# An attention, memory and expert kernel on one core: products of ones at the start, beta spread by TensorE, a shorter scaling, and tile changes counted in the plan

## The chip, the cores and the metric

The kernel runs on one core of a Trainium2 chip. The metric is the device time of one execution in microseconds, lower is better. The times of the kernel before are 636.03, 636.56 and 638.52 us; the median, 636.56 us, is the time that the change is measured against.

## The reference, cut to what matters

Four batches of eight heads, 576 positions of 64 values each, go through causal attention and, beside it, through a read of a memory matrix. A gate per head, the sigmoid of `beta`, mixes the two. The 2304 rows of 512 that come out pass through a gated expert of width 1536.

```python
a = softmax(causal(q @ k.T / 8));  local = a @ v            # 4 x 8 heads, 576 x 576, depth 64
mem_out = (phi(q) @ M_prev) / (phi(q) . z_prev + 1e-6)      # phi(x) = max(x, exp(min(x, 0)) - 1) + 1
g = 1 / (1 + exp(-beta))                                    # one number for each head
x = g * mem_out + (1 - g) * local                           # -> 2304 x 512
out = (sigmoid(x @ w_gate) * (x @ w_val)) @ w_out           # 512 -> 1536 -> 512
```

## The kernel before, in words

The 2304 rows are handled in six groups of 384 rows. Each group takes four pairs of heads, so that 24 pairs go through the attention. Group 0 and group 5 are "tail" groups: they hold the last 192 queries of two batches, with up to 576 keys; the four groups between hold the first 384 queries of one batch each.

A pair goes through these steps. `load_pair` (line 456) brings queries and keys, `load_values` (468) the values, `feature` (480) makes phi(q) on ScalarE and VectorE. `scores` (564) has TensorE multiply queries by keys: for the first nine pairs, and for one item of each pair of a tail group, through `heads` (555), which keeps 64-row tiles of the array busy side by side (fp32, line 560); for the others through split operands (line 315). VectorE adds the mask and finds the row extreme (line 597), ScalarE takes the exponential (606). `turn` (644) transposes the result, on TensorE for the first eight pairs (322), through a transposing DMA (617) between two VectorE copies (615, 619) for most of the others. `values` (666) multiplies by the values in products of 64 output rows (line 319, 66 columns), `memory` (508) does the memory read (319, 130 columns), and `scaled` (498) divides each result by its last column and multiplies it by the gate: four VectorE instructions, an addition of a small constant (501), a reciprocal (503), a product with the gate (504) and the large product (505); the helper line of the two last is 338. `across` (692) turns the mixed rows into the two halves `xh` and `xl` that the expert reads.

The expert, `moe` (818), runs over twelve slices of 128 columns of the width for each group; its matmuls are line 315. In the first group each slice's weights come from DRAM as 64-bit floats and are turned into two halves by `convert` (762) on ScalarE and VectorE (lines 769 to 780), through a ring of three landing buffers `wr`.

`gates` (376) makes the gates `gs` (the sigmoid of beta, for the memory) and `ga` (one less it, for the attention) from `bt`, a 128 x 8 tile into which one DMA (line 724) has copied the eight numbers of beta once for each partition: an exponential on ScalarE (377), an addition (378), a reciprocal (380) and a last pass (381) on VectorE.

No instruction is issued as the code is run through. Each is put in a list with its engine, a cost in microseconds and what it depends on (`Program.add`, line 80). `plan` (116) replays the list with these costs and gives every engine its order; `replay` (163) looks for time in which TensorE waits, and `issue` (198) makes 800 random trials that move late instructions forward, and keeps what is not worse. Each engine then runs its instructions strictly in the order found, SP's queue of DMAs too. In the costs, a TensorE instruction that starts before `COLD`, 8.0 us, costs half as much again, and a `heads` block carries 0.3 us on top of its columns.

```python
            if e == "pe":
                if at < COLD:
                    cost *= 1.5
```

Of the kernel before, what the change touches and what calls it, by code (L numbers as in the profile page):

```python
# [9 lines left out]
F32 = mybir.dt.float32  # L10
# [3 lines left out]
AF = mybir.ActivationFunctionType  # L14
ALU = mybir.AluOpType
# [14 lines left out]

WHEN = (20, 36)

COLD = 8.0

START = 0.7

# [15 lines left out]
class Program:  # L52
# [7 lines left out]
    def __init__(self):  # L60
        self.ops = []
        self.writer = {}
        self.readers = {}
        self.touched = {}
        self.before = {}
        self.closed = set()
        self.part = ""
        self.turn = None
        self.mates = []

    def renew(self, key):

# [43 lines left out]
    def plan(self, order):  # L116

        ops = self.ops
        left = [len(o[4]) for o in ops]
        ready_at = [0.0] * len(ops)  # L120
        engines = ["act", "dve", "pe", "pool", "sp"]
        free = dict.fromkeys(engines, START)
        link = 0.0
        coming = {e: [] for e in engines}
        ready = {e: [] for e in engines}
        for i, o in enumerate(ops):
            if not left[i]:
                heapq.heappush(coming[o[0]], (0.0, i))
        made = []
        for _ in ops:  # L130
            best = None
            for e in engines:
                if ready[e]:
                    at = free[e]
                elif coming[e]:
                    at = max(free[e], coming[e][0][0])
                else:
                    continue
                if best is None or at < best[0]:
                    best = (at, e)  # L140
            at, e = best
            while coming[e] and coming[e][0][0] <= at:
                k = heapq.heappop(coming[e])[1]
                heapq.heappush(ready[e], (order[k], k))
            i = heapq.heappop(ready[e])[1]
            _, cost, kb, _, _, _ = ops[i]
            if e == "pe":
                if at < COLD:
                    cost *= 1.5
            free[e] = at + cost  # L150
            done = free[e]
            if kb:
                link = max(link, done + WORLDS[0][1]) + kb / WORLDS[0][0]
                done = link
            made.append(i)
            for u in self.users[i]:
                ready_at[u] = max(ready_at[u], done + WAKE[e][ops[u][0]])
                left[u] -= 1
                if not left[u]:
                    heapq.heappush(coming[ops[u][0]], (ready_at[u], u))  # L160
        return made

    def replay(self, made, world):

        rate, lag, slips = world
        ops = self.ops
        ready_at = [0.0] * len(ops)
        start = [0.0] * len(ops)
        last = [-1] * len(ops)
        free = dict.fromkeys(WAKE, START)  # L170
        link = 0.0
        cold = COLD
        gaps = []
        for i in made:
            e, cost, kb, _, _, _ = ops[i]
            at = max(free[e], ready_at[i])
            if e == "pe":
                gap = at - free[e]
                if gap > 0.1:
                    gaps.append((gap, i))  # L180
                    if gap > 1.3:
                        cold = max(cold, at + 2.0)
                if at < cold:
                    cost *= 1.5
            elif e != "sp":
                cost *= slips[i]
            start[i] = at
            free[e] = done = at + cost
            if kb:
                link = max(link, done + lag) + kb / rate  # L190
                done = link
            for u in self.users[i]:
                t = done + WAKE[e][ops[u][0]]
                if t > ready_at[u]:
                    ready_at[u], last[u] = t, i
        return max(free.values()), gaps, start, ready_at, last
# [44 lines left out]
def tile_attention_memory_moe(  # L241
# [9 lines left out]
    nc = tc.nc  # L251
    B, HP, _, _ = qk.shape
# [54 lines left out]
        t, k = banks[ids[(turns[kind] - 1) % len(ids)]]  # L307
        return t, pg.renew(k)

    def pe(cost, emit, r, w):  # L310
        pg.add("pe", cost, emit, r, w)

    def matmul(out, lhsT, rhs, n, r, w, start, stop):
# [2 lines left out]

    def product(out, lhsT, rhs, n, r, w, start, stop):
        pe(0.068 if n <= 100 else 4 * n / 2385.0,
           lambda: nc.tensor.matmul(out=out, lhsT=lhsT, rhs=rhs, start=start, stop=stop), r, w)  # L319

    def transpose(out, in_, identity, r, w):
        pe(0.110, lambda: nc.tensor.transpose(out=out, in_=in_, identity=identity), r, w)  # L322
# [1 line left out]
    def act(n, emit, r, w):  # L324
        pg.add("act", 0.09 + n / 1200.0, emit, r, w)
# [4 lines left out]
    def dve(n, emit, r, w, fast=False):  # L330
        pg.add("dve", 0.065 + n / (1920.0 if fast else 960.0), emit, r, w)

    def pool(n, emit, r, w, fast=False):
        pg.add("pool", 0.2 + n / (950.0 if fast else 490.0), emit, r, w)
# [10 lines left out]
    def load(out, in_, kb, r, w):  # L345
        pg.add("sp", 0.5, lambda: nc.sync.dma_start(out=out, in_=in_), r, w, kb)
# [1 line left out]
    idn = sb.tile([128, 128], F32, name="idn")  # L348
    mask = sb.tile([128, 512], F32, name="mask")
    mask2 = sb.tile([128, 256], F32, name="mask2")  # L350
    bt = sb.tile([128, H], F32, name="bt")
    gs = sb.tile([128, H], F32, name="gs")
    ga = sb.tile([128, H], F32, name="ga")

# [19 lines left out]
            ), ["mask2"], ["mask2"])  # L374

    def gates():
        act(H, lambda: nc.scalar.activation(out=bt, in_=bt, func=AF.Exp, scale=-1.0), ["bt"], ["bt"])
        dve(H, lambda: nc.vector.tensor_scalar(
            out=gs, in0=bt, scalar1=1.0, scalar2=None, op0=ALU.add), ["bt"], ["gs"])
        dve(H * 8, lambda: nc.vector.reciprocal(out=gs, in_=gs), ["gs"], ["gs"])  # L380
        dve(H, lambda: nc.vector.tensor_scalar(
            out=ga, in0=gs, scalar1=-1.0, scalar2=1.0, op0=ALU.mult, op1=ALU.add), ["gs"], ["ga"])

    def half(t, k):
        r = slice(64, 128) if k[1] == 0 else slice(0, 64)
        pool(GT, lambda: nc.gpsimd.memset(t[r].bitcast(F32), 0.0), [], [k + ("z",)], fast=True)

    def pad(t, k):
        pool(64, lambda: nc.gpsimd.memset(t[:, S:], 0.0), [], [k + ("pad",)])
# [108 lines left out]
    def scaled(out, out_k, t, tk, ring, eps, gate, gate_k):  # L498

        r, rk = ring.take()  # L500
        dve(6, lambda: nc.vector.tensor_scalar(
            out=r, in0=t[:, :, :, D], scalar1=eps, scalar2=None, op0=ALU.add), [tk], [rk])
        dve(48, lambda: nc.vector.reciprocal(out=r, in_=r), [rk], [rk])
        tt(nc.vector, ALU.mult, r, r, gate.unsqueeze(1).to_broadcast([128, 3, 2]), 6, [rk, gate_k], [rk])
        tt(nc.vector, ALU.mult, out, t[:, :, :, :D], r.unsqueeze(3).to_broadcast([128, 3, 2, D]), GT,
           [tk, rk], out_k)

# [56 lines left out]
    def scores(n, c):  # L564
# [10 lines left out]
        def part(i, k0, k1):  # L575
            m = k1 - k0
            sp = [bank("att") for _ in js]
            if pair:
                es = [(0, 128, 0, 64), (1, 128, 64, 128)]
                mk, mk_k = (mask2[:, :m], "mask2") if i else (mask[:, :m], "mask")  # L580
            else:
                es = [(c if u.tail else 0, q0, 0, 128)]
                mk, mk_k = mask[:, 512 - W:], "mask"
            with pg.block():
                if n < SPLIT or pair:
                    pe(4 * m / 2385.0 + 0.3, lambda: heads(u, es, sp, js, k0, k1),
                       [u.kp[e][1] for e, *_ in es], [sp[j][1] for j in range(2)])
                for j in range(2) if n >= SPLIT and not pair else ():
                    for e, q, m1 in [(es[0][0], q0, 128)]:
                        kq, kk, ql, kx = u.kq[j][e]  # L590
                        keys = kq[:, u.ka + k0:u.ka + k1]
                        out, out_k = sp[j][0][:m1, :m], sp[j][1]
                        matmul(out, kq[:, u.qa + q:u.qa + q + m1], keys, m, kk, [out_k], True, False)
                        matmul(out, ql[:, q:q + m1], keys, m, kk + kx, [out_k], False, True)
            for j in range(2):
                (aj, ak), (sj, sk), (pj, pk) = a[j], st[j], sp[j]
                dve(m + 60, lambda aj=aj, sj=sj, pj=pj: nc.vector.tensor_tensor_reduce(  # L597
                    out=aj[:, k0:k1], in0=pj[:, :m], in1=mk, scale=-0.125,
                    scalar=3.0e38 if i == 0 else sj[:, i - 1:i],
                    op0=ALU.add, op1=ALU.min, accum_out=sj[:, i:i + 1],  # L600
                ), [pk, mk_k] + [sk] * (i > 0), [ak, sk])
# [115 lines left out]
    def attn():  # L717
# [3 lines left out]
        load_pair(1)  # L721
        feature(0)
        load_values(0)
        load(bt, beta.unsqueeze(0).to_broadcast([128, H]), 500, [], ["bt"])
        pg.part = "attention"
        load_values(1)
        late = []
# [167 lines left out]
    def step():  # L895
# [2 lines left out]
        pg.part = "expert"  # L898
        return y

    constants()
    a = attn()
    done = 0
# [81 lines left out]
```

## Time and profile before

| what | value |
|---|---|
| time, median of three executions | 636.56 us (636.03 to 638.52) |
| the profiled execution | 639.4 us |
| its span, first to last instruction | 637.6 us |
| TensorE matmuls busy | 620.8 us, 97% of the span |
| VectorE busy | 427.7 us, 67% |
| ScalarE busy | 301.9 us, 47% |

Busy time is the union of the recorded instructions of an engine. Matmuls overlap, so that a busy TensorE still holds short waits and slow starts. Times in the rows below count from the first instruction of the span. `PE` is TensorE's matmul, `PEld` its weight load, `DVE` VectorE, `ACT` ScalarE, `POOL` GpSimd, `SP` the engine that issues the DMAs. TensorE's two clock levels are 1.2 and 2.4 GHz; the column of the granted clock shows 1.00 for the higher one. That column is also 1.00 for a stretch ahead of the first record of the clock, so at the start the durations of matmuls of one size are the thing to read.

### The profile page before, as it was taken

The numbers are of one execution on the slowest core, as the hardware profiler recorded it, in microseconds if no ns is written. First come the engines' busy times: TensorE is split into PE (matmuls) and PEld (weight loads), VectorE is DVE, ScalarE is ACT, GpSimd is POOL, SyncE is SP. The second block draws the span as 40 slices with busy tenths as digits, with TensorE's granted clock in tenths as the row PEclk, the third lists the DMA queues.
The fourth block names the chain that finished last, engine by engine and source line by source line (L and its number), as shares of the span: only waits on it lengthen the run. The fifth ranks groups of instructions, "written<-read, shape, count | busy, mean of one in ns | idle before, by whom it ended". The sixth has DMA issues, their size and how long they took to land.

```text
span 637.6 us, 12197 instructions
## 1 busy us (share of the span) xinstructions
PE 620.8 (97%) x4740; PEld 547.2 (86%) x4740; DVE 427.7 (67%) x1164; ACT 301.9 (47%) x589; POOL 9.2 (1%) x51
## 2 busy tenths in 40 slices
PE   7989999999999989999999999999999999999997
PEld 3658888888999888899999999989898989999996
DVE  5799999999966767778767786779797422111211
ACT  5988677757743433534534643536353231221111
POOL 2000000000000000000000000000000000000000
PEclk9999999999999989999999999999999999999999
DMA  8567789895599988559867467779588433134442
GB/s 301 193 221 229 241 285 329 293 311 171 152 269 275 225 128 209 112 154 266 204 187 222 118 168 214 169 207 253 142 163 205 140 134 132 67 116 159 171 174 74
DMA packets 94362, 124.04 MB, mean 195 GB/s; under 512 B 70881, under 2 KB 72929, under 8 KB 87009
## 3 DMA queue, kind: packets, MB, share of 16 engines
q1 hardware_dynamic: 94160, 123.01, 67.8%
q8 instruction: 37, 0.61, 0.4%
q10 hardware_dynamic: 144, 0.26, 0.1%
q14 instruction: 21, 0.16, 0.1%
HBM read 89.43 MB, written 17.30 MB: 167 GB/s over the span
## 4 chain that ended last, share of the span: by engine, by line
PE 78%; DMA 10%; DVE 6%; ACT 4%; issue 1%; DVEq 0%; ACTq 0%; SPq 0%
PE bank L315 65%; PE bank L319 7%; DMA tl_wr<-pl_wr 5%; DMA wr<-in_w_dram 5%; PE bank L560 3%; PE bank L322 2%; ACT a L606 1%; ACT at L328 1%; ACT wt L769 1%; DVE wt L776 1%; DVE a L597 1%; DVE wt L773 1%; DVE pl_wr L615 1%; DVE at L619 1%; DMA kp<-in_qk_dram 0%
## 5 line engine op out<-in xcount | busy, mean ns | idle before, releaser
L315 PE MATMUL bank<-xh,wg 128*128 128x384 f32 x576 | 167.0, 343 | 0.1
L315 PE MATMUL bank<-xh,sv 128*128 128x384 f32 x576 | 163.8, 341 | 1.1 <-DVE th_a L861 1.1
L315 PE MATMUL bank<-sv,gh 128*128 128x512 f32 x432 | 138.3, 398 | 0.0
L315 PEld LDWEIGHTS bank<-xh,wg 128*128 128x128 f32 x576 | 105.9, 189 | 5.5 <-issue 0.9
L315 PEld LDWEIGHTS bank<-xh,sv 128*128 128x128 f32 x576 | 105.8, 189 | 4.0 <-issue 1.8
L861 DVE SCALAR_TENSOR_TENSOR th_a<-th_a,bank 128x384 f32<-128x384 f32 x72 | 39.7, 552 | 100.7 <-PE bank L315 99.1
L606 ACT ACTIVATE a<-a,st 128x512 f32<-128x512 f32 (+3 forms) x144 | 80.2, 584 | 41.6 <-DVE st L597 40.9
L315 PE MATMUL bank<-xl,sv 128*128 128x384 f32 x288 | 98.1, 340 | 0.0
L315 PE MATMUL bank<-xl,wg 128*128 128x384 f32 x288 | 97.9, 340 | 0.0
L315 PEld LDWEIGHTS bank<-sv,gh 128*128 128x128 f32 x432 | 79.1, 188 | 13.3 <-issue 1.7
L328 ACT CAST gh<-th_a 128x384 fp32r<-128x384 f32 x72 | 36.9, 513 | 105.8 <-DVE th_a L861 105.6
L859 ACT ACTIVATE th_a<-bank 128x384 f32<-128x384 f32 x72 | 35.2, 489 | 107.4 <-PE bank L315 107.2
L315 PE MATMUL bank<-sv,gl 128*128 128x512 f32 x216 | 85.9, 399 | 0.0
L597 DVE CUSTOM_DVE_ANT_0 a<-bank,mask 128x128 f32<-128x128 f32 (+4 forms) x144 | 66.6, 484 | 18.0 <-PE bank L560 11.8
L619 DVE COPY at<-tl_wr 128x256 uint16<-128x256 uint16 (+3 forms) x90 | 46.0, 519 | 17.4 <-DMA tl_wr<-pl_wr 17.1
L315 PEld LDWEIGHTS bank<-xl,wg 128*128 128x128 f32 x288 | 54.4, 189 | 2.8 <-issue 0.3
L315 PEld LDWEIGHTS bank<-xl,sv 128*128 128x128 f32 x288 | 54.4, 189 | 0.2
L338 DVE TENSOR_TENSOR gl<-th_a,gh 128x384 fp32r<-128x384 f32 x72 | 39.9, 555 | 13.6 <-ACT gh L328 13.0
L315 PEld LDWEIGHTS bank<-sv,gl 128*128 128x128 f32 x216 | 40.6, 188 | 9.3 <-issue 0.5
L615 DVE COPY pl_wr<-a 128x256 uint16<-128x256 uint16 (+3 forms) x90 | 41.0, 471 | 4.8 <-DMA tl_wr<-pl_wr 3.0
L328 ACT CAST kq_wt<-kp 64x768 fp32r<-64x768 f32 (+3 forms) x60 | 36.9, 614 | 12.0 <-PE bank L315 10.8
L560 PE MATMUL bank<-kp 64*64 64x320 f32 (+5 forms) x220 | 33.6, 486 | 4.9 <-DMA kp<-in_qk_dram 3.9
(75 smaller groups left out, 700.5 us busy)
## 6 DMA issues: line engine op xcount, KB each, us to landing
sv<-w SPq DMA_DIRECT2D x45, 1024.0 KB, 5.1
wr<-in_w_dram SPq DMA_DIRECT2D x36, 512.0 KB, 4.7
kp<-in_qk_dram SPq DMA_DIRECT2D x32, 384.0 KB, 4.5
w<-sv SPq DMA_DIRECT2D x12, 1024.0 KB, 7.3
out_dram<-ob SPq DMA_DIRECT2D x14, 256.0 KB, 2.4
vt<-in_vp_dram SPq DMA_DIRECT2D x8, 330.0 KB, 3.9
vr<-in_vp_dram SPq DMA_DIRECT2D x8, 330.0 KB, 4.5
mb<-in_mz_dram SPq DMA_DIRECT2D x8, 260.0 KB, 4.2
```

The lines of the kernel that those rows point to most:

```text
L315: lambda: nc.tensor.matmul(out=out, lhsT=lhsT, rhs=rhs, start=start, stop=stop), r, w)
L319: lambda: nc.tensor.matmul(out=out, lhsT=lhsT, rhs=rhs, start=start, stop=stop), r, w)
L322: pe(0.110, lambda: nc.tensor.transpose(out=out, in_=in_, identity=identity), r, w)
L328: act(n, lambda: nc.scalar.copy(out=out, in_=in_), r, w)
L338: dve(n, lambda: nc.vector.tensor_tensor(out=out, in0=in0, in1=in1, op=op), r, w)
L560: nc.tensor.matmul(out=sp[j][0][m0:m1, :k1 - k0], lhsT=kp[r, u.qa + q:u.qa + q + m1 - m0], rhs=kp[r, u.ka + k0:u.ka + k1], start=True, sto ...
L597: dve(m + 60, lambda aj=aj, sj=sj, pj=pj: nc.vector.tensor_tensor_reduce(out=aj[:, k0:k1], in0=pj[:, :m], in1=mk, scale=-0.125, scalar=3.0 ...
L606: act(W + 120, lambda aj=aj, sj=sj: nc.scalar.activation(out=aj[:, :W], in_=aj[:, :W], func=AF.Exp, scale=-1.0, bias=sj[:, len(ns) - 1:len ...
L615: dve(2 * W, lambda: nc.vector.tensor_copy(out=pl.rearrange("p (two w) -> p two w", two=2), in_=src), r, [pk], fast=True)
L619: dve(2 * W, lambda: nc.vector.tensor_copy(out=dst, in_=tl.rearrange("p (two w) -> p two w", two=2)), [lk], [key], fast=True)
L859: act(GT, lambda: nc.scalar.activation(out=th, in_=pg_[:, :GT], func=AF.Tanh, scale=0.5), [pg_k], [th_k])
L861: dve(GT, lambda: nc.vector.scalar_tensor_tensor(out=th, in0=th, scalar=1.0, in1=pv[:, :GT], op0=ALU.add, op1=ALU.mult,), [th_k, pv_k], [t ...
```

## The change

There are four parts, and a fifth that follows from them.

- `warm` puts one VectorE memset of a 128 x 128 tile of ones (in the first buffer of the ring `ob`, which the expert's outputs use later) and seven fp32 products of that tile with itself, 128 columns each, at the head of the program. They write bank 7, and nothing reads the result.
- `bt` is one row of eight numbers, loaded by a DMA of 32 bytes. `gates` multiplies a row of the ones by it on TensorE, which puts beta in all 128 rows of a PSUM bank; two ScalarE exponentials and two VectorE additions make `gs` = 1 + exp(-beta) and `ga` = 1 + exp(beta), the inverses of the gates.
- `scaled` adds the small constant and multiplies by the inverse gate in one VectorE instruction, then takes the reciprocal; the pass that multiplied by the gate is gone.
- The plan counts 0.14 us whenever TensorE goes from one tiling of the array to another (small products, two kinds of `heads`, all else); the extra of a `heads` block falls from 0.3 to 0.02 us, and `COLD` from 8.0 to 5.5 us.
- Since costs and list differ, the 800 trials start from another list, and the order of the whole program is found anew.

```diff
-COLD = 8.0
+COLD = 5.5
...
             if e == "pe":
                 if at < COLD:
                     cost *= 1.5
+                if self.modes[i] != mode:
+                    mode = self.modes[i]
+                    cost += 0.14
...
     def product(out, lhsT, rhs, n, r, w, start, stop):
         pe(0.068 if n <= 100 else 4 * n / 2385.0,
-           lambda: nc.tensor.matmul(...), r, w)
+           lambda: nc.tensor.matmul(...), r, w, int(n <= 100))
...
-    bt = sb.tile([128, H], F32, name="bt")
+    bt = sb.tile([1, H], F32, name="bt")
...
     def gates():
-        act(H, lambda: nc.scalar.activation(out=bt, in_=bt, func=AF.Exp, scale=-1.0), ["bt"], ["bt"])
-        dve(H, lambda: nc.vector.tensor_scalar(
-            out=gs, in0=bt, scalar1=1.0, scalar2=None, op0=ALU.add), ["bt"], ["gs"])
-        dve(H * 8, lambda: nc.vector.reciprocal(out=gs, in_=gs), ["gs"], ["gs"])
-        dve(H, lambda: nc.vector.tensor_scalar(
-            out=ga, in0=gs, scalar1=-1.0, scalar2=1.0, op0=ALU.mult, op1=ALU.add), ["gs"], ["ga"])
+        b, bk = bank("att")
+        one, one_k = ones.pop()
+        product(b[:, :H], one, bt, H, [one_k, "bt"], [bk], True, True)
+        for t, sign in ((gs, -1.0), (ga, 1.0)):
+            k = "gs" if t is gs else "ga"
+            act(H, lambda t=t, sign=sign: nc.scalar.activation(out=t, in_=b[:, :H], func=AF.Exp, scale=sign), [bk], [k])
+            dve(H, lambda t=t: nc.vector.tensor_scalar(
+                out=t, in0=t, scalar1=1.0, scalar2=None, op0=ALU.add), [k], [k])
...
+    def warm():
+        z, zk = ob_r.take()
+        z = z[:, :128]
+        dve(128, lambda: nc.vector.memset(z, 1.0), [], [zk], fast=True)
+        ones.append((z[:1], zk))
+        t, tk = banks[7][0], pg.renew(banks[7][1])
+        for _ in range(7):
+            product(t[:, :128], z, z, 128, [zk], [tk], True, True)
...
     def scaled(out, out_k, t, tk, ring, eps, gate, gate_k):
         r, rk = ring.take()
-        dve(6, lambda: nc.vector.tensor_scalar(
-            out=r, in0=t[:, :, :, D], scalar1=eps, scalar2=None, op0=ALU.add), [tk], [rk])
+        dve(6, lambda: nc.vector.scalar_tensor_tensor(
+            out=r, in0=t[:, :, :, D], scalar=eps, in1=gate.unsqueeze(1).to_broadcast([128, 3, 2]),
+            op0=ALU.add, op1=ALU.mult), [tk, gate_k], [rk])
         dve(48, lambda: nc.vector.reciprocal(out=r, in_=r), [rk], [rk])
-        tt(nc.vector, ALU.mult, r, r, gate.unsqueeze(1).to_broadcast([128, 3, 2]), 6, [rk, gate_k], [rk])
...
                 if n < SPLIT or pair:
-                    pe(4 * m / 2385.0 + 0.3, lambda: heads(u, es, sp, js, k0, k1),
-                       [u.kp[e][1] for e, *_ in es], [sp[j][1] for j in range(2)])
+                    pe(4 * m / 2385.0 + 0.02, lambda: heads(u, es, sp, js, k0, k1),
+                       [u.kp[e][1] for e, *_ in es], [sp[j][1] for j in range(2)], 3 if pair else 2)
...
-        load(bt, beta.unsqueeze(0).to_broadcast([128, H]), 500, [], ["bt"])
+        load(bt, beta.unsqueeze(0), 4, [], ["bt"])
...
+    warm()
     constants()
     a = attn()
```

## Rows read from the trace of the kernel before

**Rows 1.** The page: span, then busy time, share and instructions of each engine.
```profile
span 637.6 us, 12197 instructions
PE 620.8 (97%) x4740; PEld 547.2 (86%) x4740; DVE 427.7 (67%) x1164; ACT 301.9 (47%) x589; POOL 9.2 (1%) x51
```
**Rows 2.** Stretches: busy us of each engine (instructions), granted clock, DMA share, GB/s.
```profile
20.00:80.00 60.00, 56.29 (x729) 43.20 (x723) 54.67 (x165) 49.15 (x99) 1.01 (x9) 1.00 0.68 220
100.00:150.00 50.00, 48.75 (x346) 42.22 (x346) 47.29 (x113) 32.42 (x65) 0.22 (x2) 1.00 0.89 294
230.00:240.00 10.00, 10.00 (x47) 9.55 (x48) 7.05 (x21) 3.12 (x7) 0.00 (x0) 0.83 1.05 186
240.00:600.00 360.00, 359.31 (x2666) 326.31 (x2665) 220.83 (x592) 139.56 (x272) 2.71 (x13) 1.00 0.62 169
```
**Rows 3.** Waits of TensorE: for what, us in total, times, longest.
```profile
PE bank L560 <- DMA kp<-in_qk_dram: 3.9, 1, 3.9
PE bank L315 <- DVE st L597: 1.8, 1, 1.8
PE bank L315 <- DVE th_a L861: 1.1, 1, 1.1
PE bank L315 <- DVE xm L338: 1.0, 1, 1.0
```
**Rows 4.** Chain of waits, the start: start us, us, what.
```profile
0.73 3.15 DMA kp<-in_qk_dram
...
3.93 5.06 PE bank L560 x16
...
15.86 2.02 PE bank L322 x17
17.88 0.04 issue
17.92 1.38 ACT at L328 x3
```
**Rows 5.** Instructions by line and form, TensorE, first to 8.8 us, then from 9.7 us.
```profile
L560 PE MATMUL bank<-kp 64*128 64x512 f32 x8 | 3.8, 1098 | 3.9 <-DMA kp<-in_qk_dram 3.9
...
L560 PE MATMUL bank<-kp 64*128 64x512 f32 x8 | 2.6, 641 | 0.0
```
**Rows 6.** Timeline of the first microseconds: start us, us, engine, what [idle before].
```profile
0.73 0.20 POOL L356 MEMSET idn<- 128x128 f32 x1 [0.29 <-POOLq L971]
...
8.92 0.21 ACT L377 ACTIVATE bt<-bt 128x8 f32<-128x8 f32 x1 [1.30 <-DMA bt<-in_beta_dram]
9.04 0.71 ACT L606 ACTIVATE a<-a,st 128x512 f32<-128x512 f32 x1
```
**Rows 7.** DMA issues: KB each, median us from issue to landing.
```profile
kp<-in_qk_dram SPq DMA_DIRECT2D x32, 384.0 KB, 4.5
bt<-in_beta_dram SPq DMA_DIRECT2D x1, 4.0 KB, 6.8
```
**Rows 8.** Stretches at the start, columns as in rows 2.
```profile
2.00:4.00 2.00, 0.07 (x2) 0.07 (x2) 0.00 (x0) 0.10 (x2) 1.76 (x11) 1.00 0.94 321
4.00:6.00 2.00, 2.00 (x6) 0.92 (x8) 0.00 (x0) 1.15 (x3) 0.49 (x2) 1.00 0.76 199
6.00:8.00 2.00, 2.00 (x10) 0.44 (x10) 1.84 (x6) 0.73 (x2) 0.00 (x0) 1.00 0.62 234
8.00:10.00 2.00, 2.00 (x17) 0.71 (x11) 0.85 (x6) 0.85 (x3) 0.00 (x0) 1.00 1.02 404
```
**Rows 9.** Instructions by line and form, VectorE's small passes.
```profile
L338 DVE TENSOR_TENSOR rs<-rs,ga 128x6 f32<-128x6 f32 x24 | 3.9, 163 | 0.5
L338 DVE TENSOR_TENSOR rn<-rn,gs 128x6 f32<-128x6 f32 x24 | 3.9, 162 | 0.3
```
**Rows 10.** The same passes between 20 and 80 us alone.
```profile
L338 DVE TENSOR_TENSOR rs<-rs,ga 128x6 f32<-128x6 f32 x5 | 0.8, 159 | 0.0
L338 DVE TENSOR_TENSOR rn<-rn,gs 128x6 f32<-128x6 f32 x4 | 0.6, 160 | 0.0
```
**Rows 11.** Chain of waits later: VectorE's small passes, then TensorE's tile changes.
```profile
52.68 0.07 DVE rn L338
...
60.27 0.50 PE bank L319 x12
60.77 0.26 PE bank L322
61.03 2.83 PE bank L319 x92
...
119.97 0.11 PE bank L322
```
**Rows 12.** Timeline of TensorE around the long wait.
```profile
229.92 0.33 PE L315 MATMUL bank<-kq_wt 128*128 128x128 f32 x1 [1.78 <-DVE st L597]
```

More of the change, by code (lines that the diff above doesn't have):

```diff
@@ L69, in __init__ @@
         self.mates = []
+        self.modes = {}
     def renew(self, key):
@@ L129, in plan @@
         made = []
+        mode = 0
         for _ in ops:
@@ L172, in replay @@
         cold = COLD
+        mode = 0
         gaps = []
@@ L184, in replay @@
                     cost *= 1.5
+                if self.modes[i] != mode:
+                    mode = self.modes[i]
+                    cost += 0.14
             elif e != "sp":
@@ L308, in bank, with pe @@
         return t, pg.renew(k)
-    def pe(cost, emit, r, w):
+    def pe(cost, emit, r, w, mode=0):
+        pg.modes[len(pg.ops)] = mode
         pg.add("pe", cost, emit, r, w)
@@ L318, in product @@
         pe(0.068 if n <= 100 else 4 * n / 2385.0,
-           lambda: nc.tensor.matmul(out=out, lhsT=lhsT, rhs=rhs, start=start, stop=stop), r, w)
+           lambda: nc.tensor.matmul(out=out, lhsT=lhsT, rhs=rhs, start=start, stop=stop), r, w, int(n <= 100))
     def transpose(out, in_, identity, r, w):
@@ L350, in tile_attention_memory_moe @@
     mask2 = sb.tile([128, 256], F32, name="mask2")
-    bt = sb.tile([128, H], F32, name="bt")
+    bt = sb.tile([1, H], F32, name="bt")
+    ones = []
     gs = sb.tile([128, H], F32, name="gs")
```

## The prediction

> **What bounds the kernel now.** I read the page first: TensorE's matmuls fill 620.8 of 637.6 us, VectorE 427.7, ScalarE 301.9 [rows 1]. So the end is set by TensorE's work and by the time in which it does none of it or does it slowly. The table of stretches says where that is. From 240 to 600 us TensorE is busy in 359.31 of 360 us [rows 2]: nothing but fewer columns could shorten that part, and the change takes none away there. What is left stands in three places. At the start TensorE waits 3.9 us for the first keys [rows 3], and then works slowly: a 512-column instruction has a mean of 1098 ns before 8.8 us and of 641 ns from 9.7 us on [rows 5], so the clock is on its 1.2 GHz level until about 9.7 us and on 2.4 GHz afterwards, while the chain stays on TensorE from 3.93 to 17.88 us [rows 4]. From 20 to 80 us it is idle for 60.00 - 56.29 = 3.71 us, with VectorE busy in 54.67 of 60 us and ScalarE in 49.15 [rows 2]. Later there are single waits of 1.8, 1.1 and 1.0 us [rows 3]; after the longest, which ends at 229.92 us [rows 12], the granted clock of the next stretch is 0.83 [rows 2], so 0.17 x 10 = 1.7 us more are lost there.
>
> The profiled execution took 639.4 us, 637.6 of them span, and is 2.84 us above the median of 636.56. I make the sum against 639.4 and take the same difference off the median, which supposes that the fall of the clock at 230 us, for one, is not in every execution; if it is missing in most, it cannot be won there.
>
> **The products of ones.** They add one VectorE memset and seven products at the head; VectorE and TensorE have nothing else there. The nearest row of the memset is GpSimd's of the same tile, 0.20 us from 0.73 us [rows 6]; with a handover the first product starts at about 1.1 us. A product of 128 columns is a quarter of one of 512; the first stretch has eight instructions in 3.8 us, which is two items of 512 columns with two heads side by side [rows 5], so 1.9 us for one, at most 0.47 us for 128 columns at the low level, and 3.3 us for seven. They end by 4.4 us, and the first keys land at 3.88 [rows 4]. The real products stand behind them in TensorE's order, and VectorE's masks behind those: bounds 0 to 0.5 us, taken 0.2, since the 1.9 us also hold the run-out of each item.
>
> What they bring is an earlier rise. Before, TensorE worked from 3.93 to about 9.7 us, with hardly a pause, before the level rose. Now it begins to work at 1.1 us, 2.8 us sooner; if the rise comes as much sooner, 2.8 us of work at half speed become 1.4 us. More than half of the whole slow stretch, 5.8 / 2 = 2.9 us, can't be won; nothing is won if the rise stays where it was. The value taken is -1.4. The Trainium skill (TensorE: Matmul & The Clock Gate, Part 1) says that the penalty of the ramp is under 1% of a typical span, differs from run to run and should not be fitted; by 1%, an estimate from the page, up to 6.4 us could be at stake. The rows hold less than half of that, and I go by them.
>
> **Beta.** Removed: one DMA that writes eight numbers to each of 128 partitions and lands 6.8 us after its issue [rows 7]; one exponential, and three small VectorE passes. Added: a 32-byte DMA, a product of eight columns on TensorE, two exponentials, two additions. On ScalarE the exponential of beta sits at 8.92 us after 1.30 us of idle time, and the exponential of the second head, a step of the attention, stands behind it at 9.04 [rows 6]. That wait goes. It is not on the chain, which is TensorE's until 17.88 us [rows 4], so by itself it is worth 0; but it is the cover that the faster TensorE needs, since the transposes behind need those exponentials. The same holds for the transfers. They move 321 GB/s from 2 to 4 us, then 199 and 234, then 404 [rows 8]; the stretch with the beta packets loses about (321 - 199) x 2 + (321 - 234) x 2 = 418 KB, 1.0 us at 404 GB/s, and the loads behind it on SP's queue (second keys, values, weights) land up to that much earlier. I count both at nothing and name them as cover: without them the 1.4 us above would be lost to the next wait.
>
> The new wait is on TensorE: the product of beta waits for its DMA, and all matmuls behind it wait too, then VectorE's masks. If the plan puts it where the DMA is late, it costs what ScalarE lost, up to 1.3 us; if not, one small product and two tile changes, 0.2 us. Taken 0.1. A page speaks against the cure: in the Trainium skill (DMA: Bandwidth & Descriptors, Bandwidth) transfers under 64 KB are dominated by their descriptors, so 32 bytes need not land much sooner than 4 KB; no run here shows a 32-byte load yet.
>
> **The scaling.** 48 scalings lose one pass each. A pass lasts 0.163 us [rows 9] but takes 0.07 us of a packed VectorE [rows 11], so 3.4 to 7.8 us of VectorE go. The first pass takes two operands instead of one; the nearest row, the removed product itself, lasts as long as an addition does, so I take no difference (bound 0.02 us x 48 either way). It now waits for `gs`, which is ready long before any scaling. Beyond 80 us TensorE has its own work nearly always, and the pass is hidden. Between 20 and 80 us nine of these passes stand [rows 10], 0.6 to 1.5 us of VectorE, against 3.71 us of TensorE idle. ScalarE and the weights' transfers hold part of that idle time, so I take half of the upper value: -0.7 (bounds 0 and -1.5).
>
> **Tile changes.** The plan knew none; the array has them. A single transpose between two stretches of small products takes 0.26 us where one among its like takes 0.11 [rows 11]: 0.15 us for two changes. From the code there are 24 blocks of values, 8 odd memory terms and 39 `heads` blocks, 71 in all and up to 142 changes, so some 11 us. Nearly all are forced, because the blocks become ready at different times. If one in twenty-five goes, that is 0.4 us; bounds 0 and -1.5. Taken -0.4.
>
> **The order found anew** moves every wait. The waits beyond 100 us are 1.25 us in one stretch of fifty [rows 2], the one of 1.78 us at 229.92 [rows 12], another of 1.0 [rows 3], and 1.7 us of lower clock. They come from how the trials end, and the change gives the trials truer costs but no aim of its own here. I take 0, with -4 and +4 as ends.
>
> Sum: 0.2 - 1.4 + 0.1 - 0.7 - 0.4 = -2.2 us. 639.4 - 2.2 = 637.2 us for an execution like the profiled one, and 636.56 - 2.2 = 634.4 us for the median.
>
> **The rivals.**
>
> *The gain at the head is taken back.* The clock rises sooner, or does not rise sooner at all (the change then doesn't do what it says), and ScalarE, which carries the chain from 17.92 us [rows 4], ends its stretch when it did. For it: ScalarE's high share from 20 to 80 us. Against it: ScalarE's own idle time at the start was spent on beta. Left are the scaling and the tile changes, less the two added costs: -0.7 - 0.4 + 0.3 = -0.8, 635.8 us.
>
> *The new order also removes late waits.* If half of the 5.6 us beyond 100 us (1.1, 1.0, 1.8 and the 1.7 of the clock) goes too, the sum is -5.0 and the time 631.6 us. For it: the costs of TensorE come closer to the rows. Against: the waits are on VectorE, and its costs stay as they were.
>
> *The new order makes a long wait in the expert's part* (the slower end). One wait like that at 229.92 us costs 1.78 and, by the stretch after it, 1.7 us of clock: 3.5 us. One more of them than now turns -2.2 into +1.3, two more into +4.8: 641.4 us. It decides from a wait of about that length on: the stretch from 100 to 150 us holds 1.25 us of waits and shows 1.00 [rows 2]. Beta's product held for 1.3 us would add to it but not make it.
>
> **How the numbers follow.** The forecast has a chance of 0.45, the gain taken back 0.15, late waits removed 0.30, long waits made 0.10. The likeliest gives 634.4 us. The range reaches down to 630.6, one microsecond below the third case, and up to 638.6, which takes in the second case with an order that costs 2.8 us more; it leaves out 0.06 below and 0.12 above. A change of 0.5%, 3.2 us, is about what a measurement of this kernel can tell from none: under 633.4 or over 639.7. Faster has nearly all of the third case and a small part of the first, 0.34; slower most of the last and a little of the second, 0.09; the same 0.57.
>
> **What would show it.** Right: seven products from about 1.1 us to between 4.1 and 4.4; 512-column instructions at about 640 ns from 7 us on instead of 9.7; no wait of ScalarE for beta; the end of TensorE's first chain near 16.5 us; 96 small VectorE passes on six columns with reciprocals among them, instead of 144; TensorE's idle time from 20 to 80 us under 3.7 us. Wrong: a level that rises at 9.7 us as before; TensorE idle ahead of the eight-column product; a sum of idle time beyond 100 us that has moved by more than 3 us, which would make the order and not the named edits the cause.

## The result: slower by 0.6%, and the profile after

The changed kernel takes 640.21 us (median of 20 executions, 635.17 to 642.59) against 636.50 of the kernel before (20 executions, 631.98 to 638.62): ratio 1.006, 95% interval 1.0041 to 1.0079. Forecast were 634.4 us, in a range of 630.6 to 638.6. The profiled execution took 639.48 us. The ratios leave out executions more than 1.5% above the fastest of their kernel, which touches two of e1 alone, and are not quotients of the two medians.

The busy times hardly move. From the page of the changed kernel, as [rows 1]:

```profile
span 637.6 us, 12210 instructions
PE 623.6 (98%) x4756; PEld 549.7 (86%) x4756; DVE 425.1 (67%) x1116; ACT 299.0 (47%) x590; POOL 9.0 (1%) x51
```

TensorE has 16 instructions more (14 for the seven products of ones, two for beta: an fp32 product is two records) and VectorE 48 fewer. The start went as the edits intended. Timeline of the changed kernel:

```profile
0.83 0.17 DVE L406 MEMSET ob<- 128x128 f32 x1 [0.83 <-PEq L996]
...
1.05 3.36 PE L329 MATMUL bank<-ob 128*128 128x128 f32 x14 [1.05 <-DVE ob L406]
...
4.33 3.74 PE L584 MATMUL bank<-kp 64*128 64x512 f32 x16
...
8.01 0.38 PE L329 MATMUL bank<-bt,ob 1*128 1x8 f32 x2
8.09 0.71 ACT L630 ACTIVATE a<-a,st 128x512 f32<-128x512 f32 x1
```

The ones run from 1.05 to 4.41 us, the first scores start at 4.33 us instead of 3.93, and beta's product holds nobody up. Instructions of TensorE by form, first between 4.3 and 6.0 us, then between 6.4 and 12 us, as [rows 5]:

```profile
L584 PE MATMUL bank<-kp 64*128 64x512 f32 x4 | 2.0, 1092 | 0.0
...
L584 PE MATMUL bank<-kp 64*128 64x512 f32 x8 | 2.3, 641 | 0.0
```

The same instruction falls from 1092 to 641 ns at about 6 us; before, it did so at about 9.7. The chain of waits, below, leaves TensorE at 16.67 us instead of 17.88 [rows 4]: 1.2 us sooner, which is what the first two terms of the prediction add up to. It is lost again by 80 us. Stretches of the changed kernel, as [rows 2], with two short ones added:

```profile
20.00:80.00 60.00, 54.65 (x700) 41.12 (x697) 53.88 (x152) 45.06 (x93) 0.90 (x8) 0.94 0.69 216
30.00:33.40 3.40, 3.38 (x16) 0.91 (x20) 1.89 (x7) 2.72 (x5) 0.00 (x0) 0.50 0.04 16
50.50:53.90 3.40, 3.18 (x42) 2.85 (x44) 3.00 (x8) 2.99 (x6) 0.00 (x0) 0.50 0.61 180
...
240.00:600.00 360.00, 358.50 (x2623) 326.72 (x2623) 214.67 (x552) 137.37 (x270) 1.48 (x12) 1.00 0.63 167
```

Between 20 and 80 us TensorE is idle for 60.00 - 54.65 = 5.35 us, where before it was 3.71. Its clock is granted at 0.94 over that stretch instead of 1.00: twice it falls to 0.50, the lower of its two levels, for 3.4 us, which costs 1.7 us each time. VectorE and ScalarE are busy less, not more (53.88 against 54.67, 45.06 against 49.15), so the loss is not more work on either of them. From 240 to 600 us there is 1.5 us of idle time. The waits of TensorE, as [rows 3]:

```profile
PE bank L584 <- ACT at L338: 2.3, 1, 2.3
PE bank L584 <- DVE st L621: 1.4, 1, 1.4
PE bank L332 <- ACT at L338: 1.2, 2, 0.8
PE bank L329 <- DVE ob L406: 1.0, 1, 1.0
```

The longest shows what such a wait is made of. The chain of waits of the changed kernel, first where it leaves TensorE, then there (start, us, what):

```profile
15.96 0.71 PE bank L332 x5
16.67 0.02 issue
16.69 0.59 ACT at L338
...
22.56 5.29 DMA wr<-in_w_dram
...
27.93 0.66 ACT wt L793
28.60 0.51 ACT sv L338
29.10 0.38 ACT xh L338
29.48 0.50 ACT at L338
29.98 0.04 issue
30.02 1.32 PE bank L584 x5
```

and ScalarE's timeline in the same place:

```profile
25.47 0.69 ACT L793 ACTIVATE wt<-wr 128x512 f32<-128x512 f32 x1
27.93 0.66 ACT L793 ACTIVATE wt<-wr 128x512 f32<-128x512 f32 x1 [1.77 <-DVE st L621]
...
29.38 1.56 ACT L338 COPY at<-bank 128x512 f32<-128x512 f32 x3
```

ScalarE's order has the conversion of an expert weight ahead of the copies that free TensorE's banks. The weight lands at 27.85 us (22.56 + 5.29 in the chain), ScalarE is idle for 1.77 us until then (its timeline names a VectorE step, the chain the transfer), the copies stand behind the conversion, and TensorE waits 2.30 us; at 30.0 us its clock falls. None of these instructions is part of an edit. In the kernel before ScalarE waits for weights too, 0.80 us up to 31.55 and 1.19 us up to 40.88 us, but no wait of TensorE between 21 and 56 us is longer than 0.98 us there: what differs is what stands behind the conversion.

This profiled execution is not the slower one by its span, 637.6 us as before, because the profile before holds the wait and the fall of the clock at 230 us, which the new order happens not to have. The medians carry the verdict.

### The profile page after: what moved, and what is told of

Its sections match the earlier page's. It is cut to its first block, busy times and chain, and to the rows that moved or that the text cites. A ratio compares the mean times of both kernels' runs of the same rounds, so it can differ in the third digit from the quotient of the medians.

```text
span 637.6 us, 12210 instructions
## 1 busy us (share of the span) xinstructions
PE 623.6 (98%) x4756; PEld 549.7 (86%) x4756; DVE 425.1 (67%) x1116; ACT 299.0 (47%) x590; POOL 9.0 (1%) x51
## 4 chain that ended last, share of the span: by engine, by line
PE 80%; DMA 8%; DVE 6%; ACT 4%; issue 1%; ACTq 0%; SPq 0%; DVEq 0%
PE bank L325 65%; PE bank L329 10%; DMA wr<-in_w_dram 5%; PE bank L584 3%; PE bank L332 3%; DMA xs<-xm 2%; DMA tl_wr<-pl_wr 1%; ACT a L630 1%; ACT at L338 1%; ACT wt L793 1%; DVE a L621 1%; DVE wt L797 1%; DVE wt L800 1%; DVE sv L348 1%; DVE ql L348 0%
## 5 line engine op out<-in xcount | busy, mean ns | idle before, releaser
L630 ACT ACTIVATE a<-a,st 128x512 f32<-128x512 f32 (+2 forms) x144 | 79.7, 583 | 40.7 <-DVE st L621 40.1
L621 DVE CUSTOM_DVE_ANT_0 a<-bank,mask 128x512 f32<-128x512 f32 (+2 forms) x144 | 66.6, 486 | 21.1 <-PE bank L584 13.6
```

Source lines behind the costliest of these rows:

```text
L630: act(W + 120, lambda aj=aj, sj=sj: nc.scalar.activation(out=aj[:, :W], in_=aj[:, :W], func=AF.Exp, scale=-1.0, bias=sj[:, len(ns) - 1:len ...
```

## The experiments

Two theories stood after the result. *The edits*: ones, beta, or the scaling cost something of themselves. *The order*: the edits are worth what was forecast, and the order found anew costs more. They can be told apart by holding the order still. In e1 to e3 the plan sees the list of the kernel before, so that every engine gets the old order, and only what is issued differs.

| run | issued | order or costs of the plan | us (median) | ratio to before, 95% interval |
|---|---|---|---|---|
| e1 | + ones | order of before | 638.63 (637.27 of the ten in the ratio) | 1.0000 (0.9969 to 1.0031) |
| e2 | scaling less one pass | order of before | 636.11 | 0.9988 (0.9966 to 1.0009) |
| e3 | all edits | order of before | 635.07 | 0.9977 (0.9951 to 1.0003) |
| e4 | all but the ones | order of after | 639.61 | 1.0050 (1.0020 to 1.0080) |
| b_seed2 | as before | old costs, other draw | 634.81 | 0.9985 (0.9953 to 1.0016) |
| e5 | as before | new costs | 638.29 | 1.0029 (0.9999 to 1.0058) |
| e8 | as before | new costs, other draw | 638.02 | 1.0006 (0.9981 to 1.0032) |
| e6 | all edits | old costs | 631.72 | 0.9934 (0.9911 to 0.9956) |
| e7 | all edits | old costs, other draw | 635.88 | 1.0009 (0.9986 to 1.0032) |
| f1 | all edits | old costs, start 5.5 us | 634.10 | 0.9976 (0.9952 to 0.9999) |
| f2 | all edits | new costs, no charge for changes | 632.45 | 0.9942 (0.9916 to 0.9968) |
| f4 | all edits | as f2, other draw | 633.71 | 0.9933 (0.9904 to 0.9961) |
| g1 | all edits | new costs, charge 0.09 us | 634.84 | 0.9977 (0.9949 to 1.0006) |
| g3 | all edits | as g1, other draw | 635.67 | 0.9985 (0.9961 to 1.0009) |
| g2 | all edits | no charge, all TensorE costs + 3.1% | 636.15 | 0.9986 (0.9961 to 1.0011) |
| g4 | all edits | as g2, other draw | 636.92 | 1.0004 (0.9979 to 1.0029) |
| a_seed2 | all edits | new costs (charge 0.14), other draw | 639.19 | 1.0055 (1.0030 to 1.0079) |
| f3 | all edits | new costs, heads at 0.3 us | 644.31 | 1.0129 (1.0104 to 1.0154) |

The kernel before stood at 636.2 to 636.6 us beside each of these groups.

### The edits in the old order

**e1, the ones alone.**

```diff
+    z, zk = ob_r.take()
+    z = z[:, :128]
...
     with tc.manual_schedule():
+        nc.vector.memset(z, 1.0)
+        for _ in range(7):
+            nc.tensor.matmul(out=banks[7][0][:, :128], lhsT=z, rhs=z, start=True, stop=True)
         pg.issue()
```

> The order of the kernel before, kept instruction by instruction, with the memset and the seven products of ones put ahead of it. If the new order is what made the changed kernel slower (theory of the order), the ones bring what their earlier clock gives, 1 to 2 us: 634.5 to 635.5 against 636.5. If the edits themselves cost (theory of the edits) and the ones are the cause, by their delay of the first scores or by a worse place of the clock, it is slower than before, 638 or more.

No gain came, and no clear loss: the ratio is 1.0000, though its interval still takes in 1 or 2 us either way. The median of all twelve executions, 638.63 us, would meet the 638 of the second theory; that of the ten in the ratio is 637.27. The clock did rise early, at 4.9 us. The timeline of e1's profiled execution, a long one of 642.07 us, shows where the time can go:

```profile
7.87 0.66 PE L560 MATMUL bank<-kp 64*64 64x256 f32 x8
8.90 1.28 SPq L346 DMA_DIRECT2D wr<-in_w_dram  x2
8.90 0.21 ACT L377 ACTIVATE bt<-bt 128x8 f32<-128x8 f32 x1 [1.58 <-DMA bt<-in_beta_dram]
9.02 0.70 ACT L606 ACTIVATE a<-a,st 128x512 f32<-128x512 f32 x1
9.14 0.17 DVE L378 TENSOR_SCALAR gs<-bt 128x8 f32<-128x8 f32 x1 [1.43 <-ACT bt L377]
9.22 0.69 DVE L597 CUSTOM_DVE_ANT_0 a<-bank,mask 128x512 f32<-128x512 f32 x1
...
9.97 0.69 PE L560 MATMUL bank<-kp 64*128 64x512 f32 x1 [1.44 <-DVE st L597]
```

and a stretch of it right behind:

```profile
11.70:15.10 3.40, 3.40 (x15) 2.83 (x15) 1.81 (x9) 2.18 (x5) 0.47 (x4) 0.50 1.04 412
```

TensorE, now quicker, is through with its scores at 8.53 us. ScalarE waits 1.58 us for beta's slow DMA, VectorE's masks stand behind beta's addition, and TensorE waits 1.44 us for the masks. At 11.7 us its clock falls to 0.50 for 3.4 us, which costs 1.7 us. In this execution that alone is more than the 1.4 us that the prediction gave to the earlier rise.

**e2, the scaling alone.**

```diff
-        dve(H * 8, lambda: nc.vector.reciprocal(out=gs, in_=gs), ["gs"], ["gs"])
+        dve(H * 8, lambda: nc.vector.reciprocal(out=ga, in_=bt), ["gs"], ["gs"])
...
-        dve(6, lambda: nc.vector.tensor_scalar(
-            out=r, in0=t[:, :, :, D], scalar1=eps, scalar2=None, op0=ALU.add), [tk], [rk])
+        dve(6, lambda: nc.vector.scalar_tensor_tensor(
+            out=r, in0=t[:, :, :, D], scalar=eps, in1=gate..., op0=ALU.add, op1=ALU.mult), [tk], [rk])
         dve(48, lambda: nc.vector.reciprocal(out=r, in_=r), [rk], [rk])
-        tt(nc.vector, ALU.mult, r, r, gate..., 6, [rk, gate_k], [rk])
+        dve(6, lambda: None, [rk, gate_k], [rk])
```

> The order of the kernel before, with the inverse gates and one VectorE pass less in each of the 48 scalings, and nothing else. Theory of the order: the same or up to 1 us faster, 635.5 to 636.5. Theory of the edits, with the scaling as cause (its first pass slower, or its early wait for the gate): slower, 638 or more, and VectorE busy not under 425 us.

636.11 us, 0.45 us under the kernel before beside it, with an interval that holds no change; VectorE is busy 422.1 us instead of 427.7. It fits the range of the theory of the order and leaves no room for a cost of more than 0.6 us.

**e3, all edits.** The diffs of e1 and e2, and beta as one row spread by TensorE, issued where the exponential of beta stood.

> All edits to the instructions (ones, beta spread by TensorE, inverse gates, one pass less) in the order of the kernel before; only the order found anew is missing from the change. Theory of the order: 1 to 3 us faster than before, 633.5 to 635.5. Theory of the edits: as slow as the changed kernel, about 640.

635.07 us: 1.5 us faster than before, with an interval that just takes in no change, and 5.1 us faster than the changed kernel, which issues the same work. The theory of the edits falls. Whether the ones earn anything beside the new way of beta is not shown: no run has the old order and the new beta without them. Timeline of e3 at the place of the wait in e1:

```profile
6.71 0.38 PE L389 MATMUL bank<-bt,ob 1*128 1x8 f32 x2
7.02 0.77 PE L577 MATMUL bank<-kp 64*64 64x320 f32 x8
7.72 0.55 PE L332 MATMUL bank<-idn,a 128*128 128x128 f32 x3
8.20 2.15 PE L577 MATMUL bank<-kp 64*64 64x256 f32 x12
```

**e4, the order of after without the ones.**

```diff
         for _ in range(7):
-            product(t[:, :128], z, z, 128, [zk], [tk], True, True)
+            pe(4 * 128 / 2385.0, lambda: None, [zk], [tk])
```

> The order of the changed kernel, kept, without the seven products of ones. Theory of the order: slower than the changed kernel's 640.2 by the later rise of the clock, 641 to 642, and still short falls of the clock between 25 and 55 us. Theory of the edits, with the ones as cause: back towards before, 638 or less.

639.61 us. With or without the ones, the order of after is slow by about 3 us or more. The expected extra cost of taking them out did not show, nor did the falls of the clock: between 25 and 55 us the profiled execution of e4 (637.28 us) has it at 1.00, with TensorE idle for 3.67 of 30 us against 2.87 in the kernel before. So the falls are not in every execution of this order.

### What spoils the order

Two new theories: the *draw* (any new set of trials ends some microseconds off, and the kernel before had a good one) and the *costs* (the three new numbers lead the trials astray).

**e5, e6, and other draws of both kernels.** e5 is the kernel before with the new numbers and nothing else; e6 is the changed kernel with the old numbers. In b_seed2 and a_seed2 one line differs:

```diff
-        pick = random.Random(1)
+        pick = random.Random(2)
```

> The instructions of the kernel before, planned with the new costs alone (0.14 us for a change of tiling, 0.02 us for a block of heads, 5.5 us of slow start). If the new costs lead the trials to worse orders (theory of the costs): as slow as the changed kernel, 639 to 641. If any order found anew differs from the last by some microseconds either way (theory of the draw): anywhere from 633 to 641, with most of the difference from before standing between 20 and 80 us or in falls of the clock.

> All edits to the instructions, planned with the old costs. Theory of the costs: 633.5 to 635.5, as the edits in the order of the kernel before. Theory of the draw: anywhere from 632 to 640.

> The kernel before with another start of the random trials (2 for 1), and nothing else. Theory of the draw: differs from 636.5 by 1 to 4 us either way, which no edit explains. Theory of the costs: within 1 us of 636.5.

> The changed kernel with another start of the random trials (2 for 1), and nothing else. Theory of the draw: differs from 640.2 by 1 to 5 us, more likely below. Theory of the costs: 639 to 641 again.

638.29, 631.72, 634.81 and 639.19 us. The draw is worth 1.5 and 1.0 us in these two pairs, but the kernels fall in two groups by the costs, with 1.9 us between the groups (638.29 against 636.34 of the kernel before). No run decides alone: b_seed2 fits the draw only, a_seed2 fits both theories, e5 stays under the 639 of the costs, and e6 lies under both of its ranges. e6 is faster than the kernel before by 0.66% (0.44 to 0.89%) and has the lowest median of all runs here. Stretches of e6 as those above:

```profile
20.00:80.00 60.00, 56.64 (x734) 43.58 (x729) 56.88 (x163) 49.36 (x100) 1.05 (x9) 1.00 0.75 250
...
240.00:600.00 360.00, 359.83 (x2632) 328.29 (x2631) 212.76 (x551) 136.96 (x268) 2.71 (x13) 1.00 0.62 167
```

TensorE is idle for 3.36 us between 20 and 80 us, its clock stays at 1.00, and VectorE and ScalarE do more in that stretch than in the changed kernel (56.88 against 53.88, 49.36 against 45.06).

**e7, f1, f2, f3: which of the three numbers.** Each keeps all edits. e7 is e6 with another draw; f1 is e6 with `COLD` at 5.5; f2 is the changed kernel with every mode set to 0, so that no change of tiling is charged; f3 is the changed kernel with heads at 0.3 us.

```diff
-           lambda: nc.tensor.matmul(...), r, w, int(n <= 100))
+           lambda: nc.tensor.matmul(...), r, w, 0)          # f2
...
-                    pe(4 * m / 2385.0 + 0.02, ...
+                    pe(4 * m / 2385.0 + 0.3, ...             # f3
```

> All edits, old costs, as the run at 631.7 us, with another start of the random trials. Theory of the costs: again well under the kernels planned with new costs (638.3 to 640.2), 630 to 635. Theory of the draw: 631.7 was a lucky order, and this one may stand anywhere up to 640.

> All edits, old costs but the slow start of 5.5 us in place of 8.0. If the shorter slow start is the knob that spoils the order, because the plan then takes TensorE to be quicker at the start than it is: 637 or more. If it is one of the two other costs: 630 to 635.

> All edits, slow start 5.5, blocks of heads at 0.02 us, but no cost for a change of tiling: TensorE is taken to be quicker than it is. If the charge of 0.14 us is what spoils the order: 630 to 635. If the cheap heads are: 637 or more, worse than the changed kernel perhaps.

> The changed kernel with blocks of heads at 0.3 us again, so that they are counted twice: once by it and once by the changes of tiling at 0.14 us. If the charge for the changes spoils the order: 638 or more. If the cheap heads do: 630 to 635.

635.88, 634.10, 632.45 and 644.31 us. e7 is the weakest of the kernels with edits and old costs, over the range that was set for it. The shorter slow start does no harm, cheap heads without the charge do none either, and the charge with dear heads is worst. It is the charge that parts the two groups.

**f4 and e8: repeats with another draw; g1 to g4: what about the charge.** g1 has 0.09 us in place of 0.14. g2 has no charge and adds about the same total evenly, 3.1% on each TensorE cost: 18.4 us. The changed kernel's records hold 118 changes between the four kinds that the plan charges, 16.5 us, so that g2 adds slightly more than the charge does; the 132 of the expectation below counts every change of shape. g3 and g4 are their other draws.

> As the run with all edits, cheap heads and no charge (632.5 us), with another start of the random trials. If the charge is the cause: under 637 again. If that order was a lucky draw: anywhere up to 642.

> The instructions of the kernel before with the new costs, with another start of the trials. If the charge is the cause: 637.5 or more, as the run at 638.3. If the draw is: anywhere from 633 to 641.

> The changed kernel with 0.09 us in place of 0.14 for a change of tiling, which is what the traces show for one. If the charge spoils the order because it is too high: about half way back, 634 to 638. If any charge laid on the changes does: 638 or more, as with 0.14.

> All edits, no charge for changes of tiling, heads at 0.02 us, but every TensorE cost 3.1% higher: the plan gives TensorE the same total as with the charge (18.4 against 132 x 0.14 = 18.5 us), spread over all its work and not laid on the changes. If a TensorE counted too slow as a whole spoils the order: 638 or more. If it is the charge's place, on the blocks of attention in the first 100 us: 631 to 636.

> The changed kernel with 0.09 us for a change of tiling, with another start of the random trials; the first start gave 634.8 us. If the size of the charge is what matters: 632 to 637. If 634.8 was the draw: 638 or more.

> No charge, every TensorE cost 3.1% higher, with another start; the first start gave 636.2 us, between the kernels without a charge (mean 633.6) and those with 0.14 us (639.7). If the total that the plan gives TensorE is the larger part of the cause: 637 or more. If the charge's place is: under 635.

633.71 and 638.02 us for the repeats: the groups stay apart, although e8's ratio, 1.0006, does not exclude no change. With all edits, the times by what the plan charges are: no charge 631.7 to 635.9 (five kernels, mean 633.6), 0.09 us 634.8 and 635.7, the same total spread evenly 636.2 and 636.9, 0.14 us 640.2 and 639.2, 0.14 us with dear heads 644.3. The size of the charge matters, and of the 6.1 us between no charge and 0.14 us the total alone gives 2.9 (636.5 against 633.6). The other 3.2 are left for the charge's place. That follows from two draws each, beside a spread of 4 us among the five kernels without a charge, so the split is rough; g2 and g4 themselves came out between the ranges of the two explanations. For the instructions of the kernel before, the harm is not clear of the noise: 1.0029 and 1.0006 with the new costs, 0.9985 for the other draw with the old ones, and the intervals overlap.

What the charge does to an order is seen in one place, above: ScalarE's copies were left behind a conversion that waits for a DMA. That this is the way in general, a plan that takes TensorE to be busy longer and so leaves what feeds it late, was argued from that place and not shown.

## Why the prediction was wrong

**Where it failed: the order found anew, with the tile changes in its costs.** "If one in twenty-five goes, that is 0.4 us" did not happen. By shape, the records of the matmuls hold 132 changes of tiling in the kernel before, 132 in the changed one and 134 in e6; by the four kinds that the plan charges, 116, 118 and 119. `plan` does not look at the tiling when it takes the next instruction; only the trials could have kept an order for having fewer changes, and by these counts they did not. So the charge saved nothing, and its effect went into the costs by which the trials judge everything else. The next step, "the change gives the trials truer costs but no aim of its own here. I take 0", took that for harmless. With the edits held the same, the order found anew is 5.1 us slower than the old one (640.21 against 635.07), outside the bounds of 4 that were set for it; between planning with the charge and without it lie 6.1 us (639.7 against 633.6).

Nor was the charge too high where the rows give a price. The prediction read 0.15 us for two changes from the lone transpose of [rows 11], 0.26 against 0.11 us. That is the way in alone. The way back stands in the blocks of small products beside it: 12 of them take 0.50 us and 92 take 2.83, so that one takes (2.83 - 0.50) / 80 = 0.029 us and each block carries another 0.50 - 12 x 0.029 = 0.15 us. By these rows a change to or from the small products costs about 0.15 us, an estimate, and two cost 0.30 against 0.28 in the plan; for the `heads` blocks no such rows were read. The 0.09 us that an expectation gives as the traces' price is too low by the same rows, and g1 and g3, which charge it, are faster than the changed kernel. So a charge of about the size in the rows gave truer costs, as the prediction said, and worse orders all the same. Why it does so stays open: no run tells whether the plan's own sum prefers the slower orders or the 800 trials only fail to reach the better ones.

**The edits came out near their size as a whole.** In the old order they give -1.5 us (0.9951 to 1.0003, so from 3.1 us less to 0.2 us more), against -1.8 from the prediction's terms without the tile changes. How much of it each part earns is not shown. Single terms fared as follows.

- *Ones.* Forecast: end by 4.4 us, first scores 0.2 us late, rise 2.8 us sooner. Measured: 4.41, 0.40 late, and a rise about 3.5 us sooner in the profiled executions of the two kernels. In the traces the first record of the high level stands at 4.3 to 6.7 us in all 14 profiled executions with the ones and at 8.8 to 12.0 us in the six without. That the gain needs cover was also said; e1 has the ones without the new beta, and no gain. The -1.4 us by itself is shown by no run: e1 and e4 both give the ones nothing, within about 2 us. What was not foreseen is that the clock, once up, can fall again within a few microseconds (e1).
- *Beta.* ScalarE's wait of 1.30 us [rows 6] is gone in the changed kernel and TensorE does not wait at its product. The transfers that stood beside beta's gained: 199 and 234 GB/s from 4 to 8 us [rows 8] became 321 and 370 in e3. In e6 the waits of TensorE name 1.7 us of a transpose behind the second gate's exponential, more than the 1.3 that were given as the upper bound; e6 is the fastest nevertheless:

```profile
PE bank L332 <- ACT ga L394: 1.7, 1, 1.7
```

- *Scaling.* 96 passes of 0.16 to 0.19 us instead of 144, as expected. The joined pass costs no more than the addition did:

```profile
L525 DVE SCALAR_TENSOR_TENSOR rs<-bank,ga 128x6 f32<-128x6 f32 x24 | 3.9, 163 | 27.0 <-PE bank L329 27.0
L525 DVE SCALAR_TENSOR_TENSOR rn<-bank,gs 128x6 f32<-128x6 f32 x24 | 3.9, 161 | 1.3 <-PE bank L329 0.7
```

  VectorE is busy 2.6 us less in the changed kernel, a little under the lower end of 3.4, and 5.6 us less in e2, inside it; the time gained alone, 0.45 us in e2, lies in its bounds but is not told from none.

**The rivals.** The slower one named a wait that brings a fall of the clock, at 3.5 us each, and put it in the expert's part. The mechanism and the price were there (2.30 us and 1.7 at 30 us), the place was the attention of the first group, where the prediction expected idle time to shrink. Its sign of a bad order, idle time beyond 100 us that moves by more than 3 us, looked in the wrong place too: that time fell from 9.2 to 7.0 us. Over all executions the mean granted clock is 0.9957 in the changed kernel and 0.9978 in the kernel before (the 35 executions beside e1 to e4); (1 - 0.9957) x 638 = 2.7 us and (1 - 0.9978) x 635 = 1.4 us, so that by this estimate the falls make 1.3 of the 3.7 us and leave the rest to waits. The chance of slower, 0.09, was too small for a change that lets 800 random trials run on another cost.

## What to carry to other kernels

When a change alters the numbers by which a planner orders a kernel, the order is the change: hold the old order still and issue the new work in it to price the edits, and draw the order more than once to price the costs. A cost that comes closer to the trace does not make the order better by itself: here a charge of about the price in the rows gave the slowest orders, and as the changes stayed as many as before it saved nothing. An earlier rise of TensorE's clock is not yet a gain either: the ones brought it in every profiled execution, and e1 was no faster.

## What was not expected of the hardware

TensorE's clock fell to its lower level for 3.4 us after waits of 1.44 us (e1, fall at 11.7 us) and of 2.30 us (changed kernel, at 30.0 us), and stayed up in the profiled execution of e6 after one of 1.67 us that ended at 9.0 us. The second fall in the changed kernel, at 50.5 us, has no wait over 0.76 us near it (0.56, 0.44 and 0.76 us between 47 and 51 us). So the length of one wait does not settle whether it falls, against the prediction's last rival, which let it turn on a wait of about 1.8 us. Executions of one kernel differ by several microseconds: 635.17 to 642.59 for the changed kernel, with mean clocks between 0.990 and 1.000.
